# A gated linear attention followed by an ELU feed-forward layer on one core: scores and state sums in one block, and range checks at other steps

## The chip, the core and the metric

The kernel runs on one core of one Trainium2 chip. A core has a matrix engine (TensorE, PE in the profile), a vector engine (VectorE, DVE), a scalar engine (ScalarE, ACT), a general engine (GpSimd, POOL) and a sync engine (SyncE, SP) whose queue issues transfers. PE writes its products into PSUM, which this kernel divides into eight banks by name: a0 and a1 for the attention's small products, two buffers "h" for the feed-forward layer's first product, and m0 to m3 for its second. Other engines must have read a bank before PE may write it anew.

The metric is the device time of one execution in microseconds, the median of the runs.

## The reference

```
for t in range(S):                      # B, H, S, D = 4, 8, 768, 48;  f = sigmoid(f_logit)
    state = f[t] * state + outer(k[t], v[t])       # 48 x 48 for each head
    y[t]  = q[t] @ state
x = y as (B*S, H*D) = (3072, 384)
h = x @ w_in                            # 384 x 2048
g = where(h > 0, h, exp(min(h, 0)) - 1)            # ELU
return g @ w_out                        # 2048 x 384
```

The recurrence is computed by chunks of 64 tokens: inside a chunk by masked scores (k against q, then against v), between chunks by a state which is carried on. The decay f is folded into q and k beforehand. The two weights come as 64-bit floats; the kernel makes 32-bit values of them with integer operations, which is exact enough only if their sizes lie in a certain range. So it also checks that range.

## The kernel before

**Units and steps.** The 3072 tokens are twelve units of 256 (three for each batch). The feed-forward layer takes a unit in eight pairs of 128 columns of w_in, so there are 96 pairs, and the last loop runs over 192 steps T, sixteen for a unit. With P = T // 2, an even step does `up(P)`, the first product of pair P; an odd step does `joined(P)` (what is left of the first product's additions), then whatever the plan holds for this step, and then `down(P - 2)`, the second product of the pair two behind. At an even step the plan's work comes before `up`. This order of the program is the order on each engine; nothing is sorted later.

**Both products use seven instead of eight block products** from unit 1 on, in the manner of Strassen. `up7` writes two "h" buffers; DVE adds them up (L891, L904), ACT takes relu and exponential (L914, L915), DVE makes the ELU (L936, run inside the next `up7`), POOL makes sums for the second product (L946). `down` (L981) adds over the eight pairs of a unit in the banks m0 to m3; for the first pair, j = 0, it opens the banks. After the last pair ACT copies a part of m0 (L992), and DVE adds the banks up (L991): the first addition reads m3 and the copy, the second the rest of m0, then m1 and m2. These stand ahead of what follows on DVE's and ACT's queues.

**Attention** of the next unit is laid between these products by a plan, `at_step(step, ...)`. A unit u has its attention in the sixteen steps from t = 16 (u - 1), in which the feed-forward layer works on unit u - 1. A3 gives the steps after t: at 2 the transposes of k (L669, with ACT's copy, L673); at 4 `advance`, the sums that change the state (L728, banks a0 and a1); at 5 `step`, four times, DVE's addition to the state (L686); at 7 `scores` (L705, into a0 and a1) and DVE's `mask` (L713); at 9 `outputs` (L743); at 11 `carried` (L763). `advance`, `scores`, `outputs` and `carried` are blocks of 64 passes or fewer on 64 x 64 parts of the array. Unit 1 has its own list A1, unit 2 its A2. Ahead of these, DVE and POOL make the decays and scale q and k with them (L621 and L631).

**Transfers.** The loads of f, k, q and v of unit u + 1 (L438, L440, L445) are issued on SP's queue at step t. The weights' range check goes through both weights a second time in 32 parts: `reread(n)` (L595, SP's queue, 384 KB) at step 48 + 4n into one of two buffers ("again" in the profile), and `check(n)` (L603), two reductions on DVE, four steps later. Even parts are of w_in, odd ones of w_out.

**At the start** `warm` gives PE products without use (L1036).

Of the kernel before, what the change touches and what calls it, by code (L numbers as in the profile page):

```python
# [356 lines left out]
def fast(ctx: ExitStack, tc: tile.TileContext, q, k, v, f_logit, w_in, w_out, out, flag, outer):  # L357
# [18 lines left out]
    nc = tc.nc  # L376
# [7 lines left out]
    NC = U // C  # L384
    UPB = S // U
    NU = B * UPB
    HP = H // 2
    NFT = DFF // 128
# [5 lines left out]
    LAG = 2  # L394
    AHEAD = 7
    WA = 1
    F1 = (1, 3)
    W0 = 3
    HOLD = 2
    A1 = (2, 5, 6, 8, 10, 11)  # L400
    D2 = (16, 18, 20, 22)
    A2 = (23, 25, 25, 26, 27, 28)
    D3 = (-7, -5, -3, -1)
    A3 = (2, 4, 5, 7, 9, 11)
    BL = 13
    RR = 0
    MX = 10
    CB = 16
    BL1 = 13
# [176 lines left out]
    NR = 2 * NFT  # L586
# [90 lines left out]
    def step(u, c):  # L677

        if u % UPB == UPB - 1 and c == NC - 1:
            return  # L680
        new = pus[u][c % 2][:, c // 2]
        box = boxes[(u * NC + c) % len(boxes)]
        s = box[:].rearrange("n (p d) -> n p d", d=64)[:, 0:HP, PAD:]
        if u % UPB or c:
            old = sts[u, c][:].rearrange("n (p d) -> n p d", d=64)[:, 0:HP, PAD:]
            nc.vector.tensor_tensor(out=s, in0=new, in1=old, op=ALU.add)  # L686
        else:
            nc.scalar.copy(s, new)
        if c == NC - 1:
            end = qkf[u % NB]["f"][:, :, 1, U - 1 :].broadcast_to([128, HP, D])  # L690
            nc.vector.tensor_tensor(out=s, in0=s, in1=end, op=ALU.mult)
        sts[(u, c + 1) if c < NC - 1 else (u + 1, 0)] = box
# [25 lines left out]
    def advance(u, pairs=range(HP)):  # L718

        if u not in pus:  # L720
            pus[u] = [ps.tile([128, NW, HP, D], FP32, tag=n, name=f"psU{u}_{n}") for n in ("a0", "a1")]
        pu = pus[u]
        for p in pairs:
            for w in range(NW):
                for r in range(2):
                    h = 2 * p + r
                    for b in range(2):
                        nc.tensor.matmul(  # L728
                            pu[b][FULL[r], w, p], lhsT=kns[u, p // 2][FULL[b], p % 2, w, FULL[r]],
                            rhs=vs[u % NB][FULL[b], w, PAD + h * D : PAD + (h + 1) * D],  # L730
                            start=(w == 0 and p == 0), stop=(w == NW - 1 and p == HP - 1), skip_group_check=True,
                        )
# [91 lines left out]
    def at_step(step, *todo):  # L824
        plan.setdefault(step, []).extend(todo)

    def attention(u, first, then):

        kept = []
        for p, i in enumerate(first):  # L830
            at_step(i, (lambda: settle(u)) if p == NKT else lambda p=p: decays(u, p))
        if u > 1:
            at_step(then[0], lambda: transposed(u, 0, "a0"), lambda: transposed(u, 1, "a1"))
        at_step(then[1], lambda: advance(u))
        at_step(then[2], *(lambda c=c: step(u, c) for c in range(NC)))
        at_step(then[3], lambda: kept.append(scores(u)), lambda: mask(u, kept[0]))
        at_step(then[4], lambda: outputs(u))
        at_step(then[5], lambda: carried(u))

    gs, ss, pms, phs = {}, {}, {}, {}  # L840

# [108 lines left out]
    def down(P):  # L950
        m, j = order[P]
        if j == 0:
            pms[m] = [ps.tile([128, DM], FP32, tag=f"m{i + (m < DIRECT)}", name=f"psM{m}_{i}") for i in range(NW if m < DIRECT else 4)]
        pm, g = pms[m], gs.pop(P)
        ends = dict(start=(j == 0), stop=(j == NP - 1))
        if m < DIRECT:
            for i in range(2):
                for t in range(NW):
                    nc.tensor.matmul(
                        pm[t][:], lhsT=g[:, i, t * 128 : (t + 1) * 128], rhs=wo[:, 2 * j + i, :],  # L960
                        start=(j == 0 and i == 0), stop=(j == NP - 1 and i == 1),
                    )
            if j == NP - 1:
                o = (outer if (NU - m) % 2 else sb).tile([128, 2, DM], FP32, tag="o", name=f"o{m}", bufs=1)
                for t in range(NW):
                    nc.scalar.copy(o[:, t], pm[t][:])
                    t0 = m * U + t * 128
                    nc.sync.dma_start(out=out[t0 : t0 + 128, :], in_=o[:, t])
                del pms[m]
            return  # L970
        s = ss.pop(P)
        a = [[g[:, i, t * 128 : (t + 1) * 128] for i in range(2)] for t in range(2)]
        b = [[wo[:, 2 * j + i, h * DH : (h + 1) * DH] for h in range(2)] for i in range(2)]
        c = [combos[i][:, j] for i in range(4)]

        for bank, half, x, y in (
            (0, 0, a[0][0], b[0][0]), (3, 0, a[0][1], b[1][0]), (0, 1, s[:, 1], c[1]),
            (1, 0, s[:, 0], c[0]), (1, 1, s[:, 2], c[2]), (2, 1, a[1][1], c[3]), (2, 0, s[:, 3], b[1][1]),
        ):
            first = j == 0 and (bank, half) in ((0, 0), (3, 0), (1, 0), (2, 1))  # L980
            nc.tensor.matmul(  # L981
                pm[bank][:, half * DH : (half + 1) * DH], lhsT=x, rhs=y,
                start=first, stop=(j == NP - 1), skip_group_check=True,
            )
        if j == NP - 1:
            p = [[pm[i][:, h * DH : (h + 1) * DH] for h in range(2)] for i in range(4)]
            o = (outer if (NU - m) % 2 else sb).tile([128, 2, DM], FP32, tag="o", name=f"o{m}", bufs=1)
            u2 = sb.tile([128, DH], FP32, tag="u2", name=f"u2_{m}", bufs=1)
            u43 = sb.tile([128, 2, DH], FP32, tag="u43", name=f"u43_{m}", bufs=1)
            flat = o[:].rearrange("p t f -> p (t f)")  # L990
            add = lambda to, x, y: nc.vector.tensor_tensor(out=to, in0=x, in1=y, op=ALU.add)  # L991
            (nc.vector.tensor_copy if m == NU - 1 else nc.scalar.copy)(u2[:], p[0][0])  # L992
            add(flat[:, 0:DH], p[3][0], u2[:])
            add(u2[:], p[0][1], u2[:])
            add(u43[:], pm[1][:].rearrange("p (h f) -> p h f", h=2), u2[:].unsqueeze(1).broadcast_to([128, 2, DH]))
            add(flat[:, 3 * DH :], p[1][0], u43[:, 1])
            add(flat[:, DH : 3 * DH], pm[2][:], u43[:].rearrange("p h f -> p (h f)"))
            def store(*queues):
                for t in range(2):
                    for h in ((1, 0) if t else (0, 1)):  # L1000
                        queues[t].dma_start(
                            out=out[m * U + t * 128 : m * U + (t + 1) * 128, h * DH : (h + 1) * DH],
                            in_=o[:, t, h * DH : (h + 1) * DH],
                        )

            if m == NU - 1:
                left.append(store)
            else:
                store(nc.sync, nc.sync)
            del pms[m]  # L1010
# [18 lines left out]
        nc.tensor.matmul(pf[0:1, :], lhsT=low[:], rhs=causal[:, W - 1 : W], start=True, stop=True)  # L1029
        nc.vector.tensor_copy(flag[:], pf[0:1, :])  # L1030

    def warm(n, bank="m0"):

        pw = ps.tile([128, 4, 128], FP32, tag=bank, name="psW")
        for _ in range(n):
            nc.tensor.matmul(  # L1036
                pw[:], lhsT=ident[:], rhs=ident[:].unsqueeze(1).broadcast_to([128, 4, 128]), start=True, stop=True
            )
# [81 lines left out]
    at_step(F1[1], lambda: move(1, 1, nc.scalar), lambda: watch(1))  # L1120
    at_step(F1[1] + 2, lambda: scale(1, ("q", NKT, nc.gpsimd)))
    at_step(A1[0], lambda: transposed(1, 0, "a0"), lambda: transposed(1, 1, "a1"))
    attention(1, (), A1)
    at_step(8, lambda: load(2))
    at_step(14, lambda: gates(2))
# [8 lines left out]
    for u in range(3, NU):  # L1134
        t = (u - 1) * NFT
        at_step(t + BL, lambda u=u: blend(u))
        at_step(t - 16, lambda u=u: load(u))
        at_step(t - 8, lambda u=u: gates(u))
        attention(u, [t + i for i in D3], [t + i for i in A3])
    for n in range(NR):  # L1140
        t = 3 * NFT + (NU - 4) * NFT * n // NR + RR
        at_step(t, lambda n=n: reread(n))
        at_step(t + 4, lambda n=n: check(n))
    at_step((NU - 1) * NFT + 9, lambda: finish_flag(0))
    at_step((NU - 1) * NFT + 13, lambda: finish_flag(1))
    for T in range(NU * NFT):
        P = T // 2
        sevens = order[P][0] >= DIRECT
        if T % 2 and sevens:
            joined(P)  # L1150
        if T % 2 == 0 and P and order[P - 1][0] < DIRECT:
            elu(P - 1)
        for f in plan.pop(T, ()):
            f()
        if T % 2 == 0:
            up(P)
        elif P >= LAG:
            down(P - LAG)
        for n in later.pop(T, ()):
            split(n)  # L1160
            lower(n)
# [53 lines left out]
```

## Time and profile before

| | |
|---|---|
| median of 3 runs | 568.87 us (568.07 to 569.86) |
| profiled execution: span of the core | 567.3 us |
| mean granted TensorE clock in it | 0.997 |
| PE busy | 547.5 us (97%) |
| DVE busy | 409.4 us (72%) |
| POOL busy | 292.7 us (52%) |
| ACT busy | 230.2 us (41%) |
| one unit in the steady part (transposes at 173.92 and 217.66) | 43.74 us |
| scores L705, all units | 768 passes, 15.1 us busy |
| state sums L728, all units | 768 passes, 14.2 us busy |
| range checks L603 | 64 reductions, 31.7 us, 0.54 us each |

The span reaches from the first to the last instruction of the profiled execution; no other time of that execution is given, and the runs without a profile lie at their own median. A line of groups tells the line, engine and operation, the tiles written and read, the count, and the busy time. In the timeline each row has its start, its length, and at the end in brackets the idle time ahead of it with what ended it. Ends of PE's rows are modelled, so successive rows overlap by some hundredths; starts are what to compare. "issue" is a wait for which the profile has no releaser.

### The profile page before, as it was taken

The numbers are of one execution on the slowest core, as the hardware profiler recorded it, in microseconds if no ns is written. First come the engines' busy times: TensorE is split into PE (matmuls) and PEld (weight loads), VectorE is DVE, ScalarE is ACT, GpSimd is POOL, SyncE is SP. The second block draws the span as 40 slices with busy tenths as digits, with TensorE's granted clock in tenths as the row PEclk, the third lists the DMA queues.
The fourth block names the chain that finished last, engine by engine and source line by source line (L and its number), as shares of the span: only waits on it lengthen the run. The fifth ranks groups of instructions, "written<-read, shape, count | busy, mean of one in ns | idle before, by whom it ended". The sixth has DMA issues, their size and how long they took to land.

```text
span 567.3 us, 15527 instructions
## 1 busy us (share of the span) xinstructions
PE 547.5 (97%) x6336; PEld 509.7 (90%) x6336; DVE 409.4 (72%) x802; ACT 230.2 (41%) x424; POOL 292.7 (52%) x567
## 2 busy tenths in 40 slices
PE   6879998999999999999999999999999999999996
PEld 3566677999999999999999999999999999999996
DVE  8779989785675785885785885786776876745543
ACT  3287862443343433434343343333343343233331
POOL 6601788475374465456366357257248348325332
PEclk9899999999999999999999999999999999999999
DMA  8997951024024225215216216206206203201001
GB/s 212 266 261 209 298 129 43 3 47 114 3 46 138 65 52 145 79 42 156 78 36 155 86 38 153 86 19 173 84 14 178 84 6 74 84 2 36 29 2 35
DMA packets 38193, 53.30 MB, mean 94 GB/s; under 512 B 3712, under 2 KB 27936, under 8 KB 38112
## 3 DMA queue, kind: packets, MB, share of 16 engines
q1 hardware_dynamic: 37312, 51.62, 34.2%
q8 instruction: 52, 0.85, 0.7%
q10 hardware_dynamic: 800, 0.59, 0.4%
q14 instruction: 29, 0.24, 0.1%
HBM read 44.04 MB, written 4.72 MB: 86 GB/s over the span
## 4 chain that ended last, share of the span: by engine, by line
PE 81%; DMA 7%; DVE 7%; issue 2%; POOL 1%; ACT 1%; SPq 0%; DVEq 0%; ACTq 0%; POOLq 0%
PE psH L882 36%; PE psM L981 36%; DMA area<-in_moe_w_in_dram 4%; PE psS L705 2%; PE psY L743 2%; PE psY L763 2%; PE psU_a L728 2%; DVE f L631 2%; PE psT L669 1%; DMA xt<-xt 1%; DMA f<-f 1%; DVE f L626 1%; DMA k<-in_k_dram 1%; DVE bits L563 1%; DVE area L850 1%
## 5 line engine op out<-in xcount | busy, mean ns | idle before, releaser
L882 PE MATMUL psH<-xt,wi 128*128 128x128 f32 (+1 forms) x1056 | 195.0, 294 | 0.1
L946 POOL TENSOR_TENSOR sums<-gg 128x128 f32<-128x128 f32 x176 | 77.7, 462 | 214.5 <-DVE gg L936 205.9
L882 PEld LDWEIGHTS psH<-xt,wi 128*128 128x128 f32 x1056 | 149.5, 192 | 1.8 <-DVE hh L891 0.4
L914 ACT ACTIVATE gg<-hh 128x512 f32<-128x512 f32 x88 | 55.5, 631 | 232.0 <-DVE hh L904 154.6
L882 PE MATMUL psH<-xt,area 128*128 128x128 f32 x704 | 121.8, 275 | 1.3 <-DVE hh L904 1.0
L882 PEld LDWEIGHTS psH<-xt,area 128*128 128x128 f32 x704 | 106.5, 191 | 6.3 <-PE psH L882 1.3
L891 DVE TENSOR_TENSOR hh<-psH,u 128x256 f32<-128x256 f32 x88 | 37.1, 422 | 93.9 <-ACT u L889 93.9
L981 PE MATMUL psM<-area,sums 128*128 128x192 f32 x528 | 100.2, 326 | 0.0
L981 PEld LDWEIGHTS psM<-area,sums 128*128 128x128 f32 x528 | 88.2, 190 | 0.0
L981 PE MATMUL psM<-wo,gg 128*128 128x192 f32 x352 | 74.9, 335 | 0.0
L631 DVE RECIPROCAL f<-f 128x256 f32<-128x256 f32 x36 | 62.7, 1747 | 1.1
L936 DVE SCALAR_TENSOR_TENSOR gg<-gg,hh 128x512 f32<-128x512 f32 x88 | 61.9, 703 | 1.5 <-ACT gg L915 1.5
L915 ACT ACTIVATE gg<-gg 128x512 f32<-128x512 f32 x96 | 60.6, 631 | 3.0
L981 PEld LDWEIGHTS psM<-wo,gg 128*128 128x128 f32 x352 | 55.2, 190 | 2.0
L904 DVE TENSOR_TENSOR hh<-psH,u43h 128x256 f32<-128x256 f32 (+1 forms) x176 | 54.7, 352 | 3.0
L946 POOL TENSOR_TENSOR sums<-gg,sums 128x128 f32<-128x128 f32 x88 | 47.0, 534 | 6.9
L889 ACT COPY u<-psH 128x128 f32<-128x128 f32 x88 | 23.1, 263 | 60.9 <-PE psH L882 60.9
L621 POOL TENSOR_TENSOR q<-q,f 128x256 f32<-128x256 f32 x48 | 35.7, 745 | 21.8 <-DVE f L631 10.6
L904 DVE TENSOR_TENSOR u43h<-psH,hh 128x256 f32<-128x256 f32 x88 | 37.1, 422 | 12.7 <-PE psH L882 12.4
L621 POOL TENSOR_TENSOR k<-k,f 128x256 f32<-128x256 f32 x48 | 40.7, 851 | 7.1 <-DMA f<-f 5.1
L981 PE MATMUL psM<-area,gg 128*128 128x192 f32 x176 | 43.0, 326 | 0.0
L981 PE MATMUL psM<-wo,sums 128*128 128x192 f32 x176 | 43.0, 326 | 0.0
(97 smaller groups left out, 672.3 us busy)
## 6 DMA issues: line engine op xcount, KB each, us to landing
area<-in_moe_w_out_dram SPq DMA_DIRECT2D x8, 768.0 KB, 9.6
again<-in_moe_w_in_dram SPq DMA_DIRECT2D x16, 384.0 KB, 4.2
again<-in_moe_w_out_dram SPq DMA_DIRECT2D x16, 384.0 KB, 3.5
k<-in_k_dram SPq DMA_DIRECT2D x12, 384.0 KB, 4.5
q<-in_q_dram SPq DMA_DIRECT2D x12, 384.0 KB, 5.4
v<-in_v_dram SPq DMA_DIRECT2D x12, 384.0 KB, 5.8
area<-in_moe_w_in_dram SPq DMA_DIRECT2D x8, 576.0 KB, 8.4
out_dram<-o SPq DMA_DIRECT2D x42, 96.0 KB, 1.7
```

What stands on the lines that cost most here:

```text
L621: e.tensor_tensor(out=t[n][:, p], in0=t[n][:, p], in1=t["f"][:, p, "kq".index(n)], op=ALU.mult)
L631: nc.vector.reciprocal(f[:, p, 1], f[:, p, 0])
L705: nc.tensor.matmul(pc[r][FULL[b], w, p], lhsT=t["k"][FULL[r], p, cols], rhs=t["q"][FULL[r], p, cols], start=True, stop=True,)
L882: nc.tensor.matmul(to, lhsT=lhs, rhs=rhs, start=(n == 0), stop=True, skip_group_check=True)
L889: nc.scalar.copy(u1[:], pa[:, 0])
L891: add = lambda to, x, y: nc.vector.tensor_tensor(out=to, in0=x, in1=y, op=ALU.add)
L904: add = lambda to, x, y: nc.vector.tensor_tensor(out=to, in0=x, in1=y, op=ALU.add)
L914: nc.scalar.activation(g[:], h, AF.Relu, scale=-1.0)
L915: nc.scalar.activation(g[:], g[:], AF.Exp, scale=-1.0)
L936: nc.vector.scalar_tensor_tensor(out=g[:], in0=g[:], scalar=-1.0, in1=phs.pop(P), op0=ALU.add, op1=ALU.max)
L946: nc.gpsimd.tensor_tensor(out=s[:, i], in0=x, in1=y, op=op)
L981: nc.tensor.matmul(pm[bank][:, half * DH : (half + 1) * DH], lhsT=x, rhs=y, start=first, stop=(j == NP - 1), skip_group_check=True,)
```

## The change

1. **One block.** For units 3 to 7 and 9 to 11, and unit 1, `scores` and `advance` are called one after the other by a new function `both` at step t + 5. The scores go to the banks m3 and m0. Then the mask, the state sums and the four state additions follow. Unit 8 (APART) keeps its old steps (B3), unit 2 its list. A1 of unit 1 becomes 2, 6, 8, 10.
2. **Put-off second product.** At t + 5 of the joint units from 3 on, `down` of the first pair of the unit before (j = 0) isn't run; it runs at t + 7, just ahead of that of the second pair.
3. **Order of the seven products** for j = 0, in every unit with seven products: the two into bank 1, the two into bank 2, and then banks 0, 3, 0, where before it was 0, 3, 0, 1, 1, 2, 2.
4. **Range checks.** Four checks in each sixteen steps from step 48 to 175 as before (the attention of units 4 to 11), but at t, t + 1, t + 2 and t + 8, where they were at t, t + 4, t + 8 and t + 12. A transfer is issued at the step of the check two before, right after it. So the one that is checked at t is issued at t + 2 of the unit before, that for t + 1 at t + 8 of the unit before, that for t + 2 at t (behind the loads of the next unit on SP's queue), and that for t + 8 at t + 1.
5. **Small products.** At step 4 the function `warm` issues 31 products with one column into bank m3; nobody reads them.

```diff
+    SMALL = 31
-    A1 = (2, 5, 6, 8, 10, 11)
+    A1 = (2, 6, 8, 10)
-    A3 = (2, 4, 5, 7, 9, 11)
+    A3 = (2, 5, 9, 11)
+    APART, B3 = 8, (2, 4, 5, 7, 9, 11)
-    RR = 0
+    SEEN = (0, 1, 2, 8)
...
+    def both(u):
+        mask(u, scores(u, ("m3", "m0")))
+        advance(u)
+        for c in range(NC):
+            step(u, c)
...
-        at_step(then[1], lambda: advance(u))
-        at_step(then[2], *(lambda c=c: step(u, c) for c in range(NC)))
-        at_step(then[3], lambda: kept.append(scores(u)), lambda: mask(u, kept[0]))
-        at_step(then[4], lambda: outputs(u))
-        at_step(then[5], lambda: carried(u))
+        if len(then) == 4:
+            at_step(then[1], lambda: both(u))
+        else:
+            at_step(then[1], lambda: advance(u))
+            at_step(then[2], *(lambda c=c: step(u, c) for c in range(NC)))
+            at_step(then[3], lambda: kept.append(scores(u)), lambda: mask(u, kept[0]))
+        at_step(then[-2], lambda: outputs(u))
+        at_step(then[-1], lambda: carried(u))
...
-        for bank, half, x, y in (
+        todo = [
             (0, 0, a[0][0], b[0][0]), (3, 0, a[0][1], b[1][0]), (0, 1, s[:, 1], c[1]),
             (1, 0, s[:, 0], c[0]), (1, 1, s[:, 2], c[2]), (2, 1, a[1][1], c[3]), (2, 0, s[:, 3], b[1][1]),
-        ):
+        ]
+        if j == 0:
+            todo = todo[3:] + todo[:3]
+        for bank, half, x, y in todo:
...
-    def warm(n, bank="m0"):
+    def warm(n, bank="m0", small=0):
         pw = ps.tile([128, 4, 128], FP32, tag=bank, name="psW")
+        for _ in range(small):
+            nc.tensor.matmul(pw[0:1, 0, 0:1], lhsT=ident[:, 0:1], rhs=ident[:, 0:1], start=True, stop=True)
...
+    at_step(4, lambda: warm(0, "m3", SMALL))
     attention(1, (), A1)
...
-        attention(u, [t + i for i in D3], [t + i for i in A3])
+        attention(u, [t + i for i in D3], [t + i for i in (B3 if u == APART else A3)])
+    joint = [(u - 1) * NFT + A3[1] for u in range(3, NU) if u != APART]
+    seen = [(3 + n // len(SEEN)) * NFT + SEEN[n % len(SEEN)] for n in range(NR)]
     for n in range(NR):
-        t = 3 * NFT + (NU - 4) * NFT * n // NR + RR
-        at_step(t, lambda n=n: reread(n))
-        at_step(t + 4, lambda n=n: check(n))
+        at_step(seen[n], lambda n=n: check(n))
+        at_step(seen[n - 2] if n > 1 else seen[n] - 4, lambda n=n: reread(n))
...
-        elif P >= LAG:
+        elif P >= LAG and T not in joint:
+            if T - 2 in joint:
+                down(P - LAG - 1)
             down(P - LAG)
```

## The prediction

> **What bounds it.** I read first the busy lines and the chain of work that ended last, then TensorE's waits, then the stretch of one unit on each engine.
>
> ```profile
> PE 547.5 (97%) x6336; PEld 509.7 (90%) x6336; DVE 409.4 (72%) x802; ACT 230.2 (41%) x424; POOL 292.7 (52%) x567
> PE 81%; DMA 7%; DVE 7%; issue 2%; POOL 1%; ACT 1%; SPq 0%; DVEq 0%; ACTq 0%; POOLq 0%
> ```
>
> TensorE is the bound: busy for 97%. The waits of PE (waited for; total, times, longest) are few:
>
> ```profile
> PE psH L927 <- DVE wi L581: 2.3, 1, 2.3
> ...
> PE psY L808 <- issue: 1.3, 1, 1.3
> ...
> PE psS L705 <- issue: 0.7, 1, 0.7
> ```
>
> Asked for 100 to 560 us alone, the same view is empty: from the third unit on PE waits for nothing. Two transposes of successive units stand at 173.92 and 217.66, so a unit takes 43.74 us. There the time can change only by PE work taken away, or by a wait that does not exist today.
>
> **What a small block costs.** PE's timeline, first around step t+5 without a small block, then at t+7 with the scores:
>
> ```profile
> 183.00 0.39 PE L882 MATMUL psH<-xt,wi 128*128 128x128 f32 x2
> 183.22 0.82 PE L981 MATMUL psM<-wo,gg 128*128 128x192 f32 x4
> 183.88 1.14 PE L981 MATMUL psM<-area,sums 128*128 128x192 f32 x6
> ...
> 187.72 0.39 PE L882 MATMUL psH<-xt,wi 128*128 128x128 f32 x2
> 188.03 1.16 PE L705 MATMUL psS<-q,k 64*64 64x64 f32 x64
> 189.13 0.92 PE L981 MATMUL psM<-wo,gg 128*128 128x192 f32 x4
> 189.88 1.14 PE L981 MATMUL psM<-area,sums 128*128 128x192 f32 x6
> ```
>
> From L882's last group to the second L981 group: 2.16 us with the block, 0.88 without, so it costs 1.28. Its passes, once running, start 16 in 0.234 us, 0.94 for 64. The other 0.34 us is fixed: 0.09 on entry, 0.04 in the first quarter, the rest on leaving and on the first product after it. The Trainium skill ("TensorEngine Tiling (Array Packing)", Key Properties) says that changing the tiling mode drains TensorE; the trace agrees, with those 0.34 us.
>
> **The change, part by part (steady units).**
> 1. Scores and state sums stand together: one entry and exit instead of two, −0.34 us for each of eight units (3 to 7, 9, 10, 11), −2.7. Unit 1 is priced apart; unit 8 keeps its steps.
> 2. The second product put off by two steps: same instructions, two in a row at t+7. Its inputs live two steps longer: of four gg, three sums and two hh buffers exactly the last spare one is used, so no allocation waits. Priced at nothing while PE finds its banks free, which is the next point.
> 3. The scores now write banks m3 and m0 at t+5, which the previous unit's output additions (L991) still read. Before, the product that opened these banks stood at the same place. When are they free?
>
> ```profile
> 219.93 0.42 DVE L891 TENSOR_TENSOR hh<-psH,u 128x256 f32<-128x256 f32 x1 [3.26 <-ACT u L889]
> ...
> 221.18 0.42 DVE L904 TENSOR_TENSOR u43h<-psH,hh 128x256 f32<-128x256 f32 x1 [0.23 <-PE psH L882]
> ...
> 223.89 0.36 DVE L991 TENSOR_TENSOR o<-psM,u 128x192 f32<-128x192 f32 x1 [1.63 <-ACT u L992]
> ```
>
> Transposes began at 217.66. DVE's L891 comes 2.27 later, the first addition (frees m3) at 6.23, the second ends about 7.06 and frees m0. The scores would be ready when the up product of t+4 is through: its last part ends at 9.31 in this unit behind a sum block that is now gone (about 1.2), so 8.13. Slack about 1.0 us: alone the move makes no wait.
>
> 4. The range checks. Their steps go from t, t+4, t+8, t+12 to t, t+1, t+2, t+8, and the check of t+2 now reads a transfer issued only at t, right behind the four loads of the next unit on SP's queue. Before stood a transfer at that very place, and its landing can be read (SP's timeline, then the DMA issues of that stretch, last column us to landing):
>
> ```profile
> 214.63 0.46 SPq L595 DMA_DIRECT2D again<-in_moe_w_in_dram  x1
> ```
> ```profile
> again<-in_moe_w_in_dram SPq DMA_DIRECT2D x1, 384.0 KB, 6.1
> ```
>
> It lands at 220.7, 3.1 us after the transposes began. Before, its check came four steps later and never waited. DVE meets the new check at about +2.2, ahead of L891. The Trainium skill ("TensorE: Matmul & The Clock Gate", Architectural detail) calls DVE a strict first-in-first-out queue: behind the waiting check stand L891, the elu (L936), joined (L904) and the additions that free m3 and m0; ACT's copy of m0 waits behind an exponential that needs joined. No trace here shows a DMA wait in that place, so the cost is estimated. With landing L after the transposes, the check (two reductions, 1.01 us) ends at L+1.05, and L891 is late by D = L+1.05−2.27. DVE had 0.23 in hand before L904, so m0 comes free near 6.76+D against scores ready at 8.13: PE waits D−1.30 plus about 0.3, since the next up's second bank is then also set by the late DVE queue. Below L = 2.5 there is no wait. Landings read off before for units 4 to 10: 3.2, 3.1, 4.4, 4.8, 3.5, 3.8, 2.7. Unit 3 has no such check and unit 11 no next load (its transfer lands 3.0 before the transposes). The waits less the 0.34 saved (unit by unit, 3 to 11; unit 8, with its old steps, waits at a rotated product that opens with the banks freed last): −0.34, +0.68, +0.54, +1.79, +2.20, +0.86, +1.25, +0.14, −0.34. Sum +6.8. Both ends: −2.7 if no check is late, and at most +11 if each landed 0.6 later.
>
> The rotated order (banks 1, 1, 2, 2, 0, 3, 0) is the same seven products, no cost by itself. The transfers are as many and as large.
>
> **Unit 1.** POOL's scale of the last pair of q is the thing:
>
> ```profile
> 48.62 0.73 POOL L621 TENSOR_TENSOR q<-q,f 128x256 f32<-128x256 f32 x1 [5.29 <-DMA f<-f]
> ```
> ```profile
> 51.49 0.29 PE L705 MATMUL psS<-q,k 64*64 64x64 f32 x2 [0.73 <-issue]
> ```
>
> Its scores move from step 8 to 6. Without the sum block at step 5, PE would get there at 44.15, run three pairs till 45.0 and wait for q till 49.35 or a little later: 4.4 us of a new wait. Gaps of before go with it: 0.94 ahead of the scores, 0.57 ahead of L763, one block's fixed cost, and others. Following PE from there, step 16 begins 2.2 us later. From 78 to 100 us PE's listed waits sum to 2.2 (for DVE, POOL): this stretch is set by them, so most of the lateness is absorbed. I take +0.5, bounds 0 and +2.2. Granted clock: before, PE's first long wait was followed by one stretch of 3.41 us (from 24.55) at half clock; if the new one brings the same, +1.7 more at most. I leave it out of the sum.
>
> **The 31 one-column products** at step 4 (62 passes). The Trainium skill (first page named, Instruction Overhead) prices a matmul at some 60 cycles even at one column; at 25 ns each an estimate of 1.5 us. The trace shows no such form. They stand in the 2.3 us that PE waits for L581, which covers them; uncovered they cost 1.5. Taken: 0.
>
> **Sum.** 6.8 + 0.5 + 0 = +7.3 on the span of 567.3, 574.6. The median of the runs shown lies 1.6 above that span, so 576.2.
>
> **Rivals.**
> A, faster: the checks find their data. If the transfers land 0.8 to 2 us earlier than before's at the same place, D stays under 1.3 and only the merging is left: −2.7 + 0.5 = −2.2, 566.7. For: the issue order around them changes, other rereads being moved away. Against: the same four loads (about 1.4 MB) go ahead of it, and 5.7 to 7.5 us from issue to landing in seven units leave little room. It decides at L = 2.5; six of seven lie over 3.
> B, about no change: landings one us earlier, or a longer slack. Then units 6, 7 and 9 alone wait: about +0.5 + 0.5, 569.9.
> C, much slower: instruction fetch. Moving 124 PE instructions and making one block of 256 can put a fetch of the next 256 (the skill's "Runtime: NRT & Kernel Launch", Instruction fetch mechanics: 16 KiB blocks; the trace has 52 of 16 KB) inside the fastest stretch of instructions. The 1.3 us L808 wait has no other releaser. Eight such waits with the checks' would give +7 to +10 more, up to 585. Against: the merged block still needs 2.2 us for 256, and nothing after 100 us waited so.
> D: unit 1's wait costs all: 2.2 + 1.7 instead of 0.5, with the checks 579.6; without them 570.
>
> **Chances.** Mine (checks late, 573 to 579.5) 0.62; A 0.16; B with the mild form of D 0.12; C and the heavy D 0.10. A measurement of this kernel tells about 0.3% (1.7 us) from no change. Faster: A's, 0.15. Same: B's middle and A's edge, 0.09. Slower 0.76. The range from 566.4 to 579.6 holds all but C, the heavy D and the lower half of A's; mine alone is 573 to 579.5.
>
> **What would show it.** DVE's L603 would wait for the transfer "again" in units 4 to 10, 0.5 to 2.5 us each, and PE's L705 for DVE's output additions (now L1006) or ACT's copy, longest in units 6 and 7. Unit periods there would be 44 to 46 us, those of units 3 and 11 about 43.4. Near 45 us PE's L705 would wait over 4 us for POOL's L621. Wrong: if L603 waits without PE doing so, the slack was larger; if period and waits stay as they were, the transfers came early.

## The result and the profile after

The changed kernel takes 585.85 us (median of 4 runs, 583.34 to 585.87) against 568.91 (4 runs): a ratio of 1.029, 95% interval [1.0263, 1.0316]. It is slower by 17 us, where 7.3 were predicted. The profiled execution took 585.87 us, its span is 584.1 and its mean granted clock 0.99; the span of before was 567.3.

Busy time and the chain that ended last, from the page of the changed kernel:

```profile
PE 553.6 (95%) x6398; PEld 514.5 (88%) x6398; DVE 408.0 (70%) x802; ACT 228.9 (39%) x424; POOL 291.8 (50%) x567
PE 70%; DVE 10%; DMA 9%; ACT 5%; issue 4%; POOL 1%; SPq 0%; ACTq 0%; DVEq 0%; POOLq 0%
```

PE has 6 us more of busy time (among it 62 passes of small products, 1.7 us, and two stretches at half clock that are shown below), but its share of the chain has fallen from 81% to 70%; DVE, ACT and "issue" have come in. These are PE's waits (waited for; total us, times, longest):

```profile
PE psS L707 <- POOL q L623: 6.6, 3, 5.6
PE psH L894 <- DVE hh L916: 3.9, 10, 0.5
...
PE psU_a L730 <- issue: 1.9, 1, 1.9
...
PE psS L707 <- DVE u L1006: 1.4, 6, 0.2
```

and one line of DVE's:

```profile
DVE spans L605 <- DMA again<-in_moe_w_in_dram: 28.9, 7, 4.8
```

Seven times, in units 4 to 10, the range check waits for its transfer, as forecast, but for 4.1 us on average, not 0.5 to 2.5. The prediction had taken 2.2 us after the transposes for the moment at which DVE meets the check. That is when the next addition can start, which itself waits 3.26 us for ACT; DVE is free for the check 0.1 us before the transposes (unit 4, below). The cost isn't touched by this, since it was counted from the 2.27 of that addition. The periods from one unit's transposes (L671) to the next show where the time went. All were 43.7 to 43.8 us before.

| stretch | predicted | measured | period, us |
|---|---|---|---|
| start to unit 3 (transposes at 132.91, before 130.19) | +0.5 | +2.7 | |
| unit 3 | −0.34 | −0.37 | 43.38 |
| unit 4 | +0.68 | +2.25 | 46.00 |
| unit 5 | +0.54 | +1.83 | 45.58 |
| unit 6 | +1.79 | +4.39 | 48.14 |
| unit 7 | +2.20 | +0.78 | 44.53 |
| unit 8 | +0.86 | +1.28 | 45.03 |
| unit 9 | +1.25 | +2.17 | 45.92 |
| unit 10 | +0.14 | +1.59 | 45.34 |

(The measured column of units 3 to 10 is against 43.75. The stretch from unit 11's transposes to the end, −0.34 by the prediction, is 87.3 us, 0.3 more than before.) Unit 3, joined and without a late check, gains what the merging was priced at, to 0.03 us. Three things are larger than forecast: unit 1, most of the late checks, and unit 6.

**A late check, unit 4.** DVE's timeline (start, length, and in brackets the idle time ahead):

```profile
180.98 1.01 DVE L605 TENSOR_REDUCE spans<-again 128x1 f32<-128x384 f32 x2 [4.78 <-DMA again<-in_moe_w_in_dram]
181.91 0.41 DVE L903 TENSOR_TENSOR hh<-psH,u 128x256 f32<-128x256 f32 x1
...
185.54 0.36 DVE L1006 TENSOR_TENSOR o<-psM,u 128x192 f32<-128x192 f32 x1 [1.63 <-ACT u L1007]
186.01 1.02 DVE L1006 TENSOR_TENSOR u<-psM,u 128x192 f32<-128x192 f32 x2
```

and PE's, same stretch:

```profile
182.38 0.49 PE L894 MATMUL psH<-xt,wi 128*128 128x128 f32 x2 [0.34 <-DVE hh L903]
...
184.06 0.68 PE L894 MATMUL psH<-xt,area 128*128 128x128 f32 x4 [0.53 <-DVE hh L916]
...
186.51 1.10 PE L707 MATMUL psS<-q,k 64*64 64x64 f32 x59 [0.23 <-DVE u L1006]
...
189.95 0.68 PE L894 MATMUL psH<-xt,area 128*128 128x128 f32 x4 [0.27 <-DVE hh L916]
```

The transposes began at 176.28, so the transfer landed 4.70 us after them. L903 starts at 5.63 where it stood at 2.27, 3.4 us late. PE feels it at four places in turn: twice at the up product of t + 4, at the scores, whose banks L1006 frees, and at the next up product. The idle times in brackets are less than what is lost, since the ends of PE's rows are modelled. By the starts, set against the same unit in the run with checks at t + 8 and t + 12 (below), PE falls behind by 0.6, 0.7, 0.8 and 0.4 us at the four, 2.5 in all: the 2.25 of the table and what the merging saves. The shares differ from the prediction's, which put nothing at the up product of t + 4 and all but 0.3 at the scores; the sum doesn't. With the landing L of each unit as measured here (4.70, 4.28, 3.58, 3.25, 3.94, 4.64, 4.05), the prediction's formula, wait = L + 1.05 − 2.27 − 1.30 + 0.3, less 0.34 saved, gives 2.14, 1.72, 1.02, 0.69, 1.38, 2.08 and 1.49. The measured column agrees to 0.11 us in the joined units other than 6. Unit 8 is not joined; its own price (0.86 for a landing at 3.54) would be 1.26 for 3.94, and it measures 1.28.

**Unit 6.** PE stops inside the merged block, three passes before its end, for "issue":

```profile
277.92 1.08 PE L730 MATMUL psU_a<-v,kn 64*64 64x48 f32 x59
280.87 0.32 PE L730 MATMUL psU_a<-v,kn 64*64 64x48 f32 x3 [1.87 <-issue]
```

0.9 us after it the clock is halved. Busy time by window (columns: window, length, busy us of PE, PEld, DVE, ACT, POOL, then PE's clock, DMA share and GB/s):

```profile
281.81:285.22 3.41, 3.41 (x17) 3.23 (x16) 2.36 (x6) 0.31 (x2) 0.72 (x2) 0.50 0.02 5
285.22:288.60 3.38, 3.38 (x23) 3.38 (x23) 1.97 (x5) 1.89 (x3) 1.01 (x3) 1.00 0.07 7
```

1.87 us of stop and half of 3.41 us, 1.7, are 3.6; unit 6 exceeds its formula by 3.4. In the trace's list of transfers a fetch of 16 KB of PE's instructions runs from 278.00 to 279.42, the first since 256.23. PE goes on 1.45 us after it has landed.

**Unit 1.** PE's timeline at the start, and three windows around the wait:

```profile
35.21 1.69 PE L1051 MATMUL psW<-ident 128*1 128x1 f32 x62
37.58 2.83 PE L939 MATMUL psH<-xt,wi 128*128 128x256 f32 x12 [0.68 <-DVE wi L583]
40.25 2.74 PE L971 MATMUL psM<-wo,gg 128*128 128x384 f32 x8
42.92 0.93 PE L707 MATMUL psS<-q,k 64*64 64x64 f32 x48
49.45 0.71 PE L707 MATMUL psS<-q,k 64*64 64x64 f32 x16 [5.60 <-POOL q L623]
```
```profile
46.29:49.45 3.16, 0.00 (x0) 0.00 (x0) 2.48 (x4) 3.01 (x2) 0.83 (x1) 0.50 0.41 100
49.45:53.12 3.67, 3.67 (x83) 3.40 (x84) 2.28 (x5) 0.00 (x0) 0.00 (x0) 0.50 0.97 235
53.12:60.00 6.88, 6.88 (x87) 5.09 (x86) 5.93 (x11) 4.66 (x5) 0.00 (x0) 1.00 1.04 274
```

The wait is where it was forecast, but 5.6 us long, since PE came 1.2 us sooner; and the clock is halved, from within the wait, not for one stretch of 3.41 us but for two, 46.29 to 53.12, of which PE works 3.67: another 1.8 us lost. The 31 small products take 1.69 us, 27 ns a pass, and 0.68 us of the wait for the weights is left behind them: they are hidden, as assumed.

### The profile page after: what moved, and what is told of

Read it like the earlier page. It is cut to its first block, busy times and chain, and to the rows that moved or that the text cites. A ratio compares the mean times of both kernels' runs of the same rounds, so it can differ in the third digit from the quotient of the medians.

```text
span 584.1 us, 15658 instructions
## 1 busy us (share of the span) xinstructions
PE 553.6 (95%) x6398; PEld 514.5 (88%) x6398; DVE 408.0 (70%) x802; ACT 228.9 (39%) x424; POOL 291.8 (50%) x567
## 4 chain that ended last, share of the span: by engine, by line
PE 70%; DVE 10%; DMA 9%; ACT 5%; issue 4%; POOL 1%; SPq 0%; ACTq 0%; DVEq 0%; POOLq 0%
PE psM L996 31%; PE psH L894 31%; DMA again<-in_moe_w_in_dram 5%; DMA f<-f 2%; ACT area L575 2%; PE psY L745 2%; PE psY L765 2%; DMA area<-in_moe_w_out_dram 2%; DVE o L1006 1%; DVE hh L916 1%; DVE u L1006 1%; DVE f L633 1%; PE psS L707 1%; ACT gg L926 1%; PE psU_a L730 1%
## 5 line engine op out<-in xcount | busy, mean ns | idle before, releaser
L894 PE MATMUL psH<-xt,area 128*128 128x128 f32 x704 | 123.2, 277 | 4.5 <-DVE hh L916 3.9
L996 PE MATMUL psM<-area,sums 128*128 128x192 f32 x528 | 102.2, 327 | 1.1 <-DVE o L1006 1.1
L903 DVE TENSOR_TENSOR hh<-psH,u 128x256 f32<-128x256 f32 x88 | 37.0, 421 | 84.9 <-ACT u L901 84.9
L605 DVE TENSOR_REDUCE spans<-again 128x1 f32<-128x384 f32 x64 | 32.1, 543 | 28.9 <-DMA again<-in_moe_w_in_dram 28.9
```

What stands on the lines that cost most here:

```text
L605: nc.vector.tensor_reduce(out=spans[:, i, n : n + 1], in_=hi, axis=mybir.AxisListType.X, op=op, apply_absolute_value=True)
L894: nc.tensor.matmul(to, lhsT=lhs, rhs=rhs, start=(n == 0), stop=True, skip_group_check=True)
L996: nc.tensor.matmul(pm[bank][:, half * DH : (half + 1) * DH], lhsT=x, rhs=y, start=first, stop=(j == NP - 1), skip_group_check=True,)
```

## The experiments

Each time stands beside runs of the kernel before on the same chip in the same job; between jobs the medians of before are 568.5, 569.0 and 568.0.

**The late check alone, taken away.**

```diff
-    SEEN = (0, 1, 2, 8)
+    SEEN = (0, 1, 4, 8)
```

> The changed kernel with one number other: the third range check of a unit at t + 4 instead of t + 2 (the transfer before it is still issued at t). My theory (that check waits for its transfer at the head of DVE's queue, and that is what makes PE wait in units 4 to 10): the check no longer waits, each of these units loses the 0.8 to 2.3 us it had gained and its period is near 43.4 us. With the waits worked out from the landings (10.4 us in sum, and 2.0 that the merged blocks then save) it takes 573.4; if the stop of 1.9 us inside the merged block of unit 6 and the half clock after it go too, about 570. Rival (the scores in banks m3 and m0 and the second product put off are themselves what costs): it stays at 583 or more.

(By the rule of the transfers this edit also issues the one for the next unit's first check at t + 4 instead of t + 2.) Measured: 574.23 us, ratio 1.0098 [1.0074, 1.0122] to before. No check waits, nor does PE wait for DVE's output additions. The stop in unit 6 is gone with the waits, though every PE instruction stands at the same place. But the periods of units 4 to 10 are 43.75 to 43.88, not 43.4. PE's waits from 132 to 560 us, whole:

```profile
PE psH L894 <- DVE hh L916: 1.7, 7, 0.3
```

So the first theory stands in the main. From unit 3 to unit 11 this kernel takes 350.3 us, the changed one 363.9 (360.6 when it was run again): 10 to 14 us of the change are the late checks and the stop that goes with them, and the banks or the put-off product alone don't cost them. But the theory had missed something: DVE's timeline in unit 5, where the transposes began at 220.31:

```profile
228.04 0.82 DVE L1006 TENSOR_TENSOR o<-psM,u 128x192 f32<-128x192 f32 x2
228.78 1.00 DVE L605 TENSOR_REDUCE spans<-again 128x1 f32<-128x384 f32 x2
229.70 0.42 DVE L903 TENSOR_TENSOR hh<-psH,u 128x256 f32<-128x256 f32 x1
```

The check at t + 4 has its data, but stands between the output additions and the late L903 of the queue. Whether that is the 0.25 us was left to the joined version below.

**The checks' steps alone, in the kernel before.**

```diff
-        t = 3 * NFT + (NU - 4) * NFT * n // NR + RR
-        at_step(t, lambda n=n: reread(n))
-        at_step(t + 4, lambda n=n: check(n))
+        at_step(seen[n], lambda n=n: check(n))
+        at_step(seen[n - 2] if n > 1 else seen[n] - 4, lambda n=n: reread(n))
```

> The kernel before with only the range checks at the changed kernel's steps. My theory: DVE waits for the transfer as long as in the changed kernel, but the second product that opens the banks stands behind the sum block, 1.3 us later, so PE has that much more in hand. Only waits at the up products stay, 0 to 0.9 us in a unit: +2.5 to +3.5 us in all, 571.4 to 572.4. Rival (every late check costs PE what it costs DVE less a fixed slack, wherever the scores stand): +10 us or more, 579. Rival (it is the joining alone): no change, 568.9.

Measured: 571.48 us, 1.0064 [1.0038, 1.0091]: 3.0 more than before. DVE waits all but as long as in the changed kernel, and PE's listed waits are few. Of the waits of DVE and of PE from 100 to 560 us:

```profile
DVE spans L603 <- DMA again<-in_moe_w_in_dram: 26.6, 7, 4.6
```
```profile
PE psS L705 <- issue: 1.0, 2, 0.5
PE psM L981 <- DVE u L991: 0.5, 1, 0.5
```

By the starts units 4 to 10 lose 4.1 us in this profile. The size is the expected one, but the place isn't: PE waits not only at up products but first at the second product that opens the banks (L981, 0.3 us by the starts in unit 4 and 0.7 in unit 7). In this order the sum block still stands ahead of that product, 1.3 us by the prediction's price. So the same late checks cost 3 us in the one order and, after the merging is counted, over 10 in the other: the joined order had used up the slack that covered them. Which of its parts did so (the sum block gone from this place, the scores' banks, the rotated products) was not tried one by one. The two stops of 0.5 us for "issue" at the head of the scores (units 6 and 9) were in no expectation, and their cause is open.

**Unit 1 as before, the rest changed.**

```diff
-    A1 = (2, 6, 8, 10)
+    A1 = (2, 5, 6, 8, 10, 11)
```

> The changed kernel with unit 1's steps as in the kernel before (2, 5, 6, 8, 10, 11), the 31 small products kept. My theory: the 5.6 us wait for POOL's scaled q near 45 us, and the 1.8 us that the half clock costs after it, are what the changed kernel is late by from the second unit on: 2.7 us less, 583.1. Rival (as in the prediction: nearly all is taken up by later waits for DVE and POOL): 585.3.

Measured: 578.57 us, 1.0182 [1.0154, 1.0209]. That is 7.3 below the changed kernel's first median, but 3.3 below that of its repetition (next but one), where 2.7 were expected. Unit 3 begins at 128.84. The stop in unit 6 is there (1.61 us), without half clock after it.

**Fewer small products.**

```diff
-    SMALL = 31
+    SMALL = 15
```

> The changed kernel with 15 instead of 31 small products, which moves every later PE instruction 64 places against the blocks of 256 that are fetched. Theory of the fetch (the stop of 1.9 us in unit 6 comes where a fetch begins with the merged block): that stop and the half clock after it go from unit 6, 3.2 us less, 582.6, unless unit 3 or unit 7, now nearest to such a place, gets one. Rival (the stop has to do with unit 6's own waits, not with places): it stays at 585.9 with the stop in unit 6.

Measured: 580.86 us, 1.0220 [1.0189, 1.0252]. Unit 6's late check still waits (L = 3.82), its scores too, but there is no stop, and its excess of 1.35 us is the formula's 1.26. PE's waits from 262 to 313 us, whole:

```profile
PE psH L894 <- DVE hh L916: 0.5, 2, 0.3
PE psS L707 <- DVE u L1006: 0.2, 1, 0.2
```

By the order of the program (PE's weight loads, products and semaphore waits counted), a boundary of 256 instructions lies 5 instructions ahead of unit 6's block of 257 in the changed kernel, and the next one 251 inside it, which is where PE stops. Here both lie 64 places further on, the second behind the block. With the boundaries there and a late check, the stop came in four profiles of four (1.87, 1.61, 1.61 and 1.87 us: the changed kernel, its repetition, unit 1 as before, later transfers). With the boundaries there and no late check, it came in neither of two (the check at t + 4, and the checks at t + 8 and t + 12 below). With the late check and the boundaries elsewhere, it came neither here nor in any other joined unit of these five profiles. A wait of PE at the block's head isn't needed: in unit 1 as before none is listed there.

What the four have in common is in the list of transfers. PE goes on 1.26 to 1.45 us after the latest fetch of instructions has landed. In the two without a late check the fetch came sooner: it landed at 270.81 for a boundary that PE reached at 274.15, and at 269.54 for one at 272.31, and nothing stopped. So the stop goes with the landing of the fetch, and not with the place alone. Why the fetch came later where the check was late, no run shows.

**The changed kernel again.** Its text is the same.

> The changed kernel once more, beside the next three on one chip. Expected 585.9 by every theory; if the stop inside unit 6's block is a matter of chance in the fetch or in the clock, some runs lie 1.7 to 3.5 us lower.

Measured: 581.92 us (581.20 to 583.18), 1.0231 [1.0208, 1.0254], nearly 4 us below the first runs. The stop is 1.61 us and no half clock follows it (1.7 us); the landings are on average 3.86 us after the transposes instead of 4.06 (seven units, 1.4 us). So part of the first 17 us is a matter of the run: some 13 to 17 is what this change costs.

**The transfers behind the late one issued later.**

```diff
-        at_step(seen[n - 2] if n > 1 else seen[n] - 4, lambda n=n: reread(n))
+        at_step({3: seen[n] - 4, 0: seen[n] - 11}.get(n % 4, seen[n - 2]) if n > 1 else seen[n] - 4, lambda n=n: reread(n))
```

> The changed kernel with the two transfers after the late one issued later: that for the check at t + 8 at t + 4 instead of t + 1, and that for the next unit's first check at t + 5 instead of t + 2. In the changed kernel the first of them is issued about when the transposes begin, while the late transfer is still on its way. My theory (the two share the transfer engines, which is why the late one lands 0.4 us later on average than one at this place did before): the landings come 0.5 to 1 us earlier in units 4 to 10, 3 to 6 us less in all, 580 to 583. Rival (the order on the queue keeps the later one from delaying the earlier one): landings and time as in the changed kernel, 585.9.

Measured: 582.15 us, 1.0240 [1.0208, 1.0271]. Landings 3.62 us after the transposes on average, against 3.86 in the repetition, but the profile of fewer small products, which leaves the transfers as they are, has 3.66, and the checks alone 3.74. The theory is not borne out: the transfer behind does not measurably delay the one ahead. The landing varies by itself: unit 4's lies between 3.40 and 5.32 us in the four profiles that have the changed kernel's transfers and joined units (the changed kernel, its repetition, unit 1 as before, fewer small products).

**Joined, with checks that are neither late nor in the way.** Unit 1 is as before here.

```diff
-    A1 = (2, 6, 8, 10)
+    A1 = (2, 5, 6, 8, 10, 11)
-    SEEN = (0, 1, 2, 8)
+    SEEN = (0, 1, 8, 12)
```

> The changed kernel with its checks at t, t + 1, t + 8 and t + 12, so that none waits for its transfer and none stands between t + 2 and t + 7, and unit 1 as in the kernel before. In the run with the check at t + 4 the period was 43.87 us; my reading is that this check stands ahead of the late additions on DVE and PE waits 0.25 us for these in each unit. Expected: periods of 43.4 us in all joined units, 565.5 us in all, 3 us less than before. Rival (the waits of 0.25 us come from the two second products in a row or from the scores' banks): periods stay near 43.9 and the time near 569.

Measured: 566.80 us, 0.9968 [0.9952, 0.9984]. All joined units have periods of 43.38 or 43.39 us, unit 8 has 43.75, and PE waits nowhere from 132 to 560 us. So the 0.25 us (and the rest of the 0.5 us per unit) came from the checks' steps. Two were moved, and of these it is the one at t + 4 that stood in the way on DVE's timeline. The joining itself is worth its 0.36 us a unit. Neither the put-off product nor the scores' banks cost anything here. PE's timeline in unit 5:

```profile
227.07 1.16 PE L707 MATMUL psS<-q,k 64*64 64x64 f32 x64
228.06 1.10 PE L730 MATMUL psU_a<-v,kn 64*64 64x48 f32 x64
229.09 0.49 PE L894 MATMUL psH<-xt,wi 128*128 128x128 f32 x2
```

It takes 2.0 us from the first score to the next up product.

**The same without small products** (`SMALL` and its step left out).

> The kernel of the run above (checks at t, t + 1, t + 8, t + 12; unit 1 as before) without the 31 small products. If these stand in the wait for the weights, as the trace of the changed kernel shows (1.7 us of them and then 0.7 us of wait), the time is the same within 0.5 us, about 565.5. Rivals: 1 to 1.5 us less, where they cost what they take; or more, where the first fetches or the clock come off worse without them.

Measured: 566.21 us, 0.9964 [0.9948, 0.9979]: no difference that can be told, they are hidden. One unit (4) has a stop of 0.6 us for "issue" in its sums, with no wait ahead of it:

```profile
180.45 0.98 PE L730 MATMUL psU_a<-v,kn 64*64 64x48 f32 x54
182.06 0.37 PE L730 MATMUL psU_a<-v,kn 64*64 64x48 f32 x10 [0.64 <-issue]
```

Counted as above, a boundary of 256 instructions lies at this pass too, and the fetch had landed 1.34 us before PE went on.

**Unit 1 joined, nothing else.** The joint steps, put-off products, order and checks are as before.

```diff
-    A1 = (2, 5, 6, 8, 10, 11)
+    A1 = (2, 6, 8, 10)
```

> The kernel before with only unit 1's scores and sums joined at its step 6 (2, 6, 8, 10), nothing else of the change. Over five profiles each, unit 3 began at 133.5 us with these steps and at 129.4 with the old ones. My theory now (the wait for POOL's scaled q, and the half clock that follows it, are not taken up by later waits): about 4 us more, 573. Rival (as in the prediction, later waits take it up): +0.5, 569.5. In between, about +2, if it is the wait alone and the half clock does not come.

Measured: 572.43 against 567.99 us, 1.0070 [1.0044, 1.0096], 4.4 us more. Unit 3 begins at 133.72, before at 130.19. PE's waits of before from 78 to 100 us, which the prediction took to absorb the lateness, and those of this run from 40 to 103.5, by which time it is 3.5 us late:

```profile
PE psH L882 <- DVE hh L904: 1.0, 2, 0.5
PE psT L669 <- POOL k L621: 0.9, 1, 0.9
PE psH L882 <- DVE gg L936: 0.3, 1, 0.3
```
```profile
PE psS L707 <- POOL q L623: 4.5, 1, 4.5
PE psT L671 <- POOL k L623: 0.8, 1, 0.8
PE psH L894 <- DVE gg L948: 0.6, 1, 0.6
PE psH L894 <- DVE hh L916: 0.5, 1, 0.5
```

The later waits still stand at 1.9 us of 2.2; they have taken up little. Starts differ from run to run, but over all profiles unit 3 begins at 127.7 to 132.2 us with unit 1's old steps (six) and at 132.9 to 134.7 with the new ones (six). The clock is halved from 47.87 us for 6.83 us, as in the changed kernel.

**Unit 8 joined too** (on the version without small products; APART names no unit).

> The kernel with checks at t, t + 1, t + 8, t + 12, unit 1 as before and no small products, and unit 8 joined like the others. If nothing in unit 8 is different, its period goes from 43.75 to 43.39 us and the time is 0.4 less, about 565.8. Rival (unit 8 was left out because joining it costs there, by a fetch or a wait): its period is 44 or more.

Measured: 566.53 us, 0.9967 [0.9950, 0.9983] to a before of 567.99. Unit 8's period is 43.39, as expected; the median does not show it. In unit 4 this program is that of the run without small products, but here the fetch landed 1.88 us before PE reached the same boundary, and there is no stop.

**And unit 1 joined at step 8.**

```diff
-    A1 = (2, 5, 6, 8, 10, 11)
+    A1 = (2, 8, 10, 11)
```

> The kernel of the run above, and unit 1 joined at step 8, where its scores stood before and POOL's scaled q (ready near 49.4 us) is there. If the cost of joining unit 1 is only that wait, this costs nothing and saves the fixed part of one block and some of the 0.9 us gap there: 565 to 565.8. Rival (joining unit 1 costs in itself, by the later state sums): 567 or more.

Measured: 566.53 us, 0.9962 [0.9946, 0.9978]. That lies between the two expectations. Unit 3 begins at 128.82 us, and at 128.80 in the run above: joining unit 1 costs nothing there, nor does it gain, so its cost at step 6 was the wait for q with the half clock that came with it. Unit 9 has a stop in its sums, 0.37 us by the list and 0.6 by the starts, again at such a boundary and 1.29 us after a fetch had landed.

## Why the prediction was wrong

The direction was right, and so were the mechanism of the late checks and its place; the size was not: 16.9 us for 7.3, and the time lies above the range. Three terms of the sum failed: the landings were taken as fixed, unit 1's lateness was taken as absorbed, and the fetch of instructions was put at nothing.

- **Merging, −0.34 us per unit.** Right: −0.37 in unit 3, 43.38 or 43.39 us in the joined units of the last versions, but for the two with a stop.
- **The late check.** Right as a mechanism, and the working from landing to PE's wait holds to 0.1 us in units 4, 5 and 7 to 10. Mis-sized was its input: the landings were taken from one profile of before, 3.6 us after the transposes on average. Here they were 4.06, and the sum of the seven units 10.5 instead of 7.5. In the four other profiles of the changed checks in joined units the average is 3.6 to 3.9 (7.4 to 9.1 us by the formula), so over two thirds of that excess is the spread of a transfer. The prediction's +11 for later landings covers it, but was not carried into the range. The forecast that units 6 and 7 would be the longest was read off the same single profile, and was wrong. (In the working, 6.76 for the freeing of m0 should read 6.83, that is 7.06 less 0.23; the 1.30 that follows is right.)
- **Unit 1, +0.5.** The step that failed: "most of the lateness is absorbed". The joining of unit 1 alone costs over 4 us. The listed waits of 2.2 us from 78 to 100 us, for DVE and POOL, moved along with PE: in the run with unit 1 alone 1.9 of them are still there, 3.5 us later. The half clock was priced at 1.7 and left out of the sum without a reason: it came in each of six profiles with this wait, for 6.83 us in five of them and for 3.41 in one. The Trainium skill ("TensorE: Matmul & The Clock Gate", Part 1) gives an idle window of about 3.4 us as its cause; here the 5.6 us wait brought 6.83 us at 0.5. Rival D's price, 2.2 + 1.7 = 3.9, is close to what was measured.
- **Fetch, rival C.** Given 0.10 with the heavy form of D, for eight units; it came in one, 1.9 us of stop and 1.7 of half clock. The reason given against it, that nothing after 100 us waited so before, was too weak: a block that runs its 256 instructions in 2.0 us stops when the fetch lands late, and that was seen in unit 6 here, in unit 4 without the small products and in unit 9 of the last run. The prediction's suspicion of the 1.3 us at L808 was sound: that wait stands at a boundary too, 1.7 us after a landing.
- **Small products, 0; rotated order, 0; put-off product, 0.** Right where no check is late: then no PE wait is left, and leaving the small products out changes nothing. With a late check the rotated order isn't free, as the prediction allowed for in unit 8. Unit 8, with the old steps and the rotated order, lost 1.28 us at a landing of 3.94; with the checks alone, not rotated, unit 4 lost 0.64 at 4.08 and unit 7 1.04 at 4.48. The rotated order was not tried alone.
- **Rival A** fell (all seven transfers landed over 3 us after the transposes, 3.25 to 4.70). About 567 us is what the joining gives, but with other steps for the checks.

The sum with the measured parts: 2.7 (unit 1 in this pair of profiles) + 10.5 (checks) + 3.4 (unit 6) − 0.37 (unit 3) = 16.2 of the 16.8 us between the spans. The 3.4 is what unit 6 has over its formula, not a price worked out ahead.

What stays open: why a fetch of instructions came later in unit 6 where the check was late, and what the two stops of 0.5 us in single blocks of the checks-alone run were.

## What to carry to other kernels

Price a wait at the head of an in-order queue by what is behind it, and by the slack of its readers: the same seven late checks cost 3 us where a block stood ahead of the readers and over 10 in the joined order. Read the landing of a transfer from several profiles before a slack of about 1 us is built on it. A wait of PE of 4.5 us or more cost its length here and half of what PE did in the half-clock stretch that came with it; later waits of PE for DVE and POOL gave back 0.3 us of it. A block that packs 256 instructions of PE into 2 us has little room for a late fetch; where its boundary falls can be counted from the program.

## What the runs showed of the hardware

- A wait of 4.5 to 5.9 us brought 6.83 us at half clock in five profiles of six, and 3.41 in the sixth; in the changed kernel PE worked in 3.67 us of the 6.83. A wait of 3.1 us for ACT (unit 1, in the run with checks at t + 8 and t + 12) was followed by 3.41 us at half clock. A stop of 1.87 us was followed by 3.41 us at half clock in one profile of four; three stops of 1.6 to 1.9 us were not.
- One-column 32-bit products took 27 ns a pass (62 in 1.69 us).
- A fetch of PE's instructions can stop it in the steady part, for 0.4 to 1.9 us. That came six times, in three units, each time at a boundary of 256 instructions near the end of a block of 257 that otherwise runs in 2.0 us. PE went on 1.26 to 1.45 us after the fetch had landed. At no boundary after 125 us in all thirteen traces (some 40 in each) did PE go on sooner than 1.26 us after the landing.
